# One tile for all of PSUM and a new order of work in a fused attention and MLP-mixer kernel

## The chip, the cores and the metric

The kernel runs on one core of a Trainium2 chip. The core has five engines that run their own instruction streams: TensorE (PE in the profile; its weight loads are listed as PEld), VectorE (DVE), ScalarE (ACT), GpSimd (POOL) and SyncE (SP). The metric is the device time of one execution in microseconds (us), lower is better. Before the change it is 283.89 us, the median of three runs (283.52, 283.89 and 284.70).

## The reference

The inputs are q, k and v with 8 batches, 8 heads, 576 positions and head size 64, and four weight matrices. A blockwise causal attention comes first: a position sees all positions of its own block of 64 and of earlier blocks. Its output, with the heads side by side (576 x 512 for each batch), goes through an MLP mixer: first over positions, then over channels.

```python
scores = scale * np.matmul(q, k.transpose(0, 1, 3, 2))
mask = block_i >= block_j                       # blocks of 64 positions
attn = np.exp(scores masked, less the row's maximum)
attn = attn / np.sum(attn, axis=-1, keepdims=True)
x = np.matmul(attn, v)                          # heads side by side: 8 x 576 x 512
h = np.maximum(x.transpose(0, 2, 1) @ w_tok1, 0.0) @ w_tok2   # 576 -> 256 -> 576
u = x + h.transpose(0, 2, 1)
out = u + np.maximum(u @ w_ch1, 0.0) @ w_ch2                  # 512 -> 1536 -> 512
```

## The kernel before, in words

Each batch goes through the same stages. The q and k of four heads (a head group) are loaded and turned by VectorE in 32x32 blocks (`STREAM_TRANSPOSE`, L440), so that the head dimension lies on the partitions. TensorE makes the scores from 32 rows at a time (`score_set`, L562). ScalarE takes the exponential: for the first batch over a pair of PSUM banks at once (`exp`, L580) or over one bank (L736), for later batches over one bank (L777). VectorE or GpSimd clear the masked corners (`clear`, L599) and copy a tail (L588). TensorE multiplies with v (`head_out`, L616, and `ends_out` for the last 64 positions, L669), and VectorE divides by the sums: a reciprocal and a multiply (L636 and L642, or L691 and L697). A column of ones beside v gives the sums.

Then comes the mixer: `token_up` (L814, L818, the ReLU after it at L800 or L802), for the first batch `first_u` (L849), an add of x (L862), a transpose by TensorE (L874) with the copy behind it (L393 on ScalarE, L395 on VectorE), `channel_up` (L1041) and the way back down. Other batches use forms with fewer multiplications whose lines play no part in the change.

The work is not written in the order in which it runs. Functions add operations to a list (class `Plan`, `P.add`), each with its engines, dependencies and the PSUM banks that it takes and gives back. A table of words, `ORDER` (L97 to L175), then says in which order they are issued, on which engine, and with which banks: `105Ts` is operation 105 on TensorE in the pair of banks called s, `106A` operation 106 on ScalarE. `placed()` goes through the table and emits. The engines run each its own part of that order, and wait for each other by semaphores. There are 1526 operations that are always emitted or may be.

Of PSUM's eight banks the kernel uses four as single tiles (`mm`, letters a to d) and four as two pairs (`sc`, letters s and t) for the first batch's scores. After the last pair's exponential, operation 166, the pairs are closed and four single tiles (`late`, letters e to h) opened in their place; operation 166 therefore depends also on all earlier pair exponentials.

A set of operations does nothing for the output: `raise_clock` multiplies zeros by zeros on TensorE. The first does it eleven times, 512 columns wide (L364). Another 37 (L372), of which every fourth is 256 columns wide and the others 512, may be put anywhere in the first 20 us or left out: the kernel before emits 25 of them.

GpSimd issues the loads of q, k, v and of the weights in its own order, between its other instructions: q and k (L435, L417), v (L469, one load per 128 positions, for the first batch in two head groups of five loads), the three token weights of which `w1o_sb` is a small remainder of the first (L480), and the channel weights (L503, L512). In this queue an issue sometimes waits until a load issued some places earlier has landed. The identity that TensorE's transposes use is made by GpSimd as well (masks.py).

## Time and profile before

| what | value |
| --- | --- |
| time, median of 3 runs | 283.89 us |
| span of the profiled execution | 282.2 us |
| TensorE busy | 275.3 us (98%), 3580 matmuls |
| VectorE busy | 238.8 us (85%) |
| ScalarE busy | 177.8 us (63%) |
| GpSimd busy | 78.8 us (28%) |
| moved by DMA | 31.75 MB |

The profile is of one execution; it gives its span, from the first to the last instruction, and no other time of that execution. The span is 1.7 us below the median of the runs, which also hold what lies around it. In timelines a row is a group of instructions: its start and length in us, engine, line, operation, and the result and the operands by their tiles' names; in brackets stands how long its engine was idle before it, and what ended that.

### The profile page before, as it was taken

How to read it: one execution, taken by the hardware profiler on the slowest of the kernel's cores; microseconds unless marked ns; L12 is line 12 of the kernel's file. 1: busy time of each engine (PE TensorE's matmuls, PEld its weight loads, DVE VectorE, ACT ScalarE, POOL GpSimd, SP SyncE). 2: the span in 40 equal slices, each digit the busy share in tenths (PEclk: the TensorE clock that was granted, in tenths of full speed). 3: DMA queues.
4: the chain of work that ended last, by engine and by line, in shares of the span. 5: the costliest groups of instructions: out<-in, count | busy, mean ns of one | idle time of the engine just before them, and what ended most of it. 6: DMA issues, size and time to landing. Idle time of an engine off the chain costs nothing.

```text
span 282.2 us, 8544 instructions
## 1 busy us (share of the span) xinstructions
PE 275.3 (98%) x3580; PEld 193.2 (68%) x3580; DVE 238.8 (85%) x523; ACT 177.8 (63%) x326; POOL 78.8 (28%) x131
## 2 busy tenths in 40 slices
PE   7899999999999999999999999999999999999994
PEld 2457665475768877888776658744589664788884
DVE  4589598889889989999988879887797898898974
ACT  4788888775899774899997990326840858530000
POOL 8876726371613422092257210000000000000000
PEclk9999999999999999999999999999999999999999
DMA  8999999959958947699399465150127200020555
GB/s 160 167 153 194 191 200 203 162 63 170 95 88 229 150 67 56 151 104 127 46 118 161 31 141 120 42 114 19 37 49 210 80 0 0 3 75 14 212 126 174
DMA packets 64918, 31.75 MB, mean 112 GB/s; under 512 B 53104, under 2 KB 56176, under 8 KB 64880
## 3 DMA queue, kind: packets, MB, share of 16 engines
q0 software_dynamic: 45040, 17.64, 54.0%
q1 hardware_dynamic: 19408, 12.91, 16.7%
q10 hardware_dynamic: 432, 0.66, 0.7%
q8 instruction: 28, 0.46, 0.7%
q14 instruction: 10, 0.08, 0.1%
HBM read 35.85 MB, written 9.44 MB: 160 GB/s over the span
## 4 chain that ended last, share of the span: by engine, by line
PE 82%; DMA 10%; DVE 3%; ACT 2%; POOL 1%; issue 1%; DVEq 0%; POOLq 0%
PE mm L1372 13%; PE late L1372 11%; DMA qk_sb<-in_q_dram 7%; PE late L1114 7%; PE late L1238 6%; PE mm L1114 6%; PE mm L1238 6%; PE mm L562 4%; PE late L616 3%; DMA wc_sb<-in_moe_w_ch_dram 3%; PE late L562 3%; PE late L913 3%; PE mm L814 2%; PE mm L616 2%; PE late L814 2%; PE mm L913 2%
## 5 line engine op out<-in xcount | busy, mean ns | idle before, releaser
L777 ACT ACTIVATE e_sb<-mm 128x512 bf16<-128x512 f32 x94 | 53.5, 612 | 9.8 <-PE mm L562 4.2
L777 ACT ACTIVATE e_sb<-late 128x512 bf16<-128x512 f32 x74 | 43.0, 613 | 5.6 <-PE late L562 2.7
L440 DVE STREAM_TRANSPOSE qk_sb<-qk_sb 128x288 int32<-128x288 int32 (+2 forms) x57 | 38.3, 695 | 6.0 <-ACT qk_sb L393 1.9
L469 POOL DMA_DIRECT2D vals<-in_v_dram x45 | 37.1, 833 | 8.5 <-PE late L616 7.5
L1372 PEld LDWEIGHTS <-sums 128*128 128x128 bf16 x288 | 27.8, 98 | 4.2 <-issue 0.4
L1372 PEld LDWEIGHTS <-gT 128*128 128x128 bf16 x288 | 27.9, 98 | 3.7
L562 PEld LDWEIGHTS <-qk_sb 32*64 32x64 bf16 (+1 forms) x1024 | 16.9, 99 | 16.5 <-issue 9.6
L562 PE MATMUL mm<-qk_sb 32*64 32x320 bf16 (+6 forms) x534 | 27.7, 273 | 0.0
L616 PEld LDWEIGHTS <-e_sb 128*128 128x128 bf16 x640 | 23.9, 97 | 5.4 <-issue 0.9
L393 ACT COPY late<-mm 128x512 f32<-128x512 f32 (+1 forms) x14 | 8.0, 571 | 27.6 <-DVE o_sb L1396 14.5
L562 PE MATMUL late<-qk_sb 32*64 32x320 bf16 (+6 forms) x382 | 25.0, 277 | 0.3 <-DVE x_sb L642 0.3
L1114 PEld LDWEIGHTS <-ws_sb 128*128 128x128 bf16 x192 | 17.9, 98 | 4.2 <-issue 0.9
L599 POOL MEMSET e_sb<- 64x512 bf16 (+1 forms) x23 | 11.4, 511 | 31.7 <-ACT e_sb L777 28.4
L800 ACT ACTIVATE gT<-late 128x512 bf16<-128x512 f32 x20 | 12.2, 611 | 7.4 <-PE late L1114 4.9
L1114 PEld LDWEIGHTS <-wc_sb 128*128 128x128 bf16 x144 | 15.5, 113 | 1.8
L1238 PEld LDWEIGHTS <-ws_sb 128*128 128x128 bf16 x96 | 9.4, 98 | 9.8
L616 PE MATMUL late<-vals,e_sb 128*128 128x65 bf16 x360 | 15.8, 193 | 0.0
L642 DVE TENSOR_TENSOR x_sb<-late,rinv 128x256 bf16<-128x256 f32 x36 | 14.8, 418 | 0.7
L580 ACT ACTIVATE e_sb<-sc 128x1024 bf16<-128x1024 f32 x11 | 10.8, 1026 | 4.5 <-PE sc L562 4.5
L1372 PE MATMUL mm<-wd_sb,sums 128*128 128x256 bf16 x108 | 13.1, 273 | 0.0
L616 PE MATMUL mm<-vals,e_sb 128*128 128x65 bf16 x280 | 12.4, 193 | 0.0
L417 POOL DMA_DIRECT2D qk_sb<-in_k_dram x12 | 6.6, 551 | 20.7 <-ACT e_sb L777 7.1
(203 smaller groups left out, 649.4 us busy)
## 6 DMA issues: line engine op xcount, KB each, us to landing
out_dram<-o_sb SPq DMA_DIRECT2D x14, 512.0 KB, 3.0
vals<-in_v_dram POOLq DMA_DIRECT2D x28, 128.0 KB, 5.9
qk_sb<-in_k_dram POOLq DMA_DIRECT2D x12, 288.0 KB, 5.6
qk_sb<-in_q_dram POOLq DMA_DIRECT2D x12, 288.0 KB, 6.1
wc_sb<-in_moe_w_ch_dram POOLq DMA_DIRECT2D x8, 192.0 KB, 7.8
wc_sb<-in_moe_w_ch_dram POOLq DMA_DIRECT2D x3, 512.0 KB, 8.0
out_dram<-o_sb SPq DMA_DIRECT2D x4, 256.0 KB, 3.2
vals<-in_v_dram POOLq DMA_DIRECT2D x15, 64.0 KB, 5.4
```

The costliest lines, as they stand in the source:

```text
L440: nc.vector.transpose(dst[:, 0:S, :] .rearrange("p s e -> p (s e)") .bitcast(I32) .rearrange("p (a k) -> p k a", k=NB)[:, k0:k1], raw2.bit ...
L469: nc.gpsimd.dma_start(out=t[128 - p : 128, J, hs, 0:64], in_=src)
L562: nc.tensor.matmul(out=home(n)[rows, c : c + w], lhsT=kT[i][r, 64 * j : 64 * j + keys, par], rhs=qT[i][r, 64 * q : 64 * q + w, par], start ...
L599: (nc.vector if o.engine == "DVE" else nc.gpsimd).memset(late_keys, 0.0)
L616: nc.tensor.matmul(out=u[:, I, 0:65], lhsT=e[:, h, c : c + 128], rhs=vt[:, J, head, 0:65], start=(J == 0), stop=(J == I),)
L642: nc.vector.tensor_tensor(out=xt[:, 0:4, 64 * head : 64 * head + 64], in0=u[:, :, 0:64], in1=ri[:, 0:4].to_broadcast([128, 4, 64]), op=MULT,)
L777: nc.scalar.activation(dst, bank_of(x), EXP, scale=scale)
L800: nc.scalar.activation(dst, src, RELU)
L913: nc.tensor.matmul(out=bank_of(bank), lhsT=w2_sb[:, t, 128 * si : 128 * si + 128], rhs=at[:, t, :], start=(t == 0), stop=(t == NDT - 1),)
L1114: nc.tensor.matmul(out=bank_of(bank)[:, 256 * o_ : 256 * o_ + 256], lhsT=x(o_, m), rhs=y[:, :, m, :], start=opens, stop=m == 1, skip_group ...
L1238: nc.tensor.matmul(out=bank_of(bank), lhsT=x(m), rhs=y[:, :, m, :], start=first and m == 0, stop=m == 1, skip_group_check=not first,)
L1372: nc.tensor.matmul(out=bank_of(bank)[:, 256 * i : 256 * i + 256], lhsT=x[:, kk, 128 * i : 128 * i + 128], rhs=y[:, kk], start=first and i ...
```

## The change

PSUM becomes a single tile of eight banks. A word names the bank by letters a to h; a first-batch pair takes any two neighbouring banks. The bookkeeping of pools goes, and so do operation 166's extra dependencies. The core of the diff:

```diff
-    mm = ring(4, [128, 512], FP32, "mm", psum)
-    held_banks = [tc.tile_pool(name="pairs", bufs=1, space=bass.MemoryType.PSUM)]
-    sc = ring(2, [128, 2, 512], FP32, "sc", held_banks[0].__enter__())
-    late = []
+    banks_sb = psum.tile([128, 8, 512], FP32, name="banks")
...
-    def bank_of(note):
-        if note["pool"] in EARLY:
-            return mm[note["slot"]]
-        if not late:
-            held_banks[0].__exit__(None, None, None)
-            held_banks[0] = tc.tile_pool(name="singles", bufs=1, space=bass.MemoryType.PSUM)
-            late.extend(ring(4, [128, 512], FP32, "late", held_banks[0].__enter__()))
-        return late[note["slot"]]
+    def bank_of(note, i=0):
+        return banks_sb[:, note["slot"] + i]
...
-            nc.scalar.activation(dst, sc[SC.index(note["pool"])][:, :, 0:n], EXP, scale=scale)
+            nc.scalar.activation(dst, banks_sb[:, note["slot"] : note["slot"] + 2, 0:n], EXP, scale=scale)
...
-                    late_banks = [{"pool": "late", "covers": True, "slot": i} for i in range(4)] if (j, n) == (3, 2) else None
-                    these = [exp(dst, 512, op, note, prio + 0.1 * n, urgent=2, give=late_banks, after=seen if late_banks else [])]
+                    these = [exp(dst, 512, op, note, prio + 0.1 * n, urgent=2)]
```

The table `ORDER` is written anew throughout; its first lines before and after:

```diff
-    13D 26D 24D 105Ts 106A 98Ttbc 61Td 57Td 49Td 99A 100D 30D 63Td 118A 122Ts 70Td 123A 78Td 62Td 54Td 102Tt 103A
+    22D 13D 26D 24D 43Ta 44Ta 45Ta 30D 67Ta 82P 47Ta 34P 35P 72Tg 76Tf 57Tf 70Th 32P 55Tf 48Tb 28D 59Tc 105Tc
```

The operations are the same apart from the warming ones, of which 30 in place of 25 are emitted behind the first eleven. Of the small operations that more than one engine can do, 38 go from VectorE to ScalarE, 34 the other way, 12 from VectorE to GpSimd and 9 the other way.

TensorE up to the first scores (L562 before, L527 after; `wd_sb` holds the zeros of the warming matmuls, L372 before, L343 after). The end of the warming before, and the first scores:

```order
L372 LDWEIGHTS wd_sb
L372 MATMUL mm<-wd_sb 128x512
L372 LDWEIGHTS wd_sb
L372 MATMUL mm<-wd_sb 128x512
L562 LDWEIGHTS qk_sb
L562 MATMUL sc<-qk_sb 128x512
```

and after:

```order
L343 LDWEIGHTS wd_sb
L343 MATMUL banks<-wd_sb 128x256
L343 LDWEIGHTS wd_sb
L343 MATMUL banks<-wd_sb 128x512
L343 LDWEIGHTS wd_sb
L343 MATMUL banks<-wd_sb 128x512
L343 LDWEIGHTS wd_sb
L343 MATMUL banks<-wd_sb 128x512
L527 LDWEIGHTS qk_sb
L527 MATMUL banks<-qk_sb 128x512
```

Four of these optional matmuls stand ahead of the first scores before, sixteen after; behind them come twenty-one before and fourteen after.

VectorE around the first adds of batch 0's mixer (L862 before, L824 after), whose results TensorE transposes. Before:

```order
L440 STREAM_TRANSPOSE qk_sb<-gT 128x9x32 x2
L636 RECIPROCAL rinv<-late 128x4
L642 TENSOR_TENSOR x_sb<-late,rinv 128x4x64
L440 STREAM_TRANSPOSE qk_sb<-gT 128x9x32
L636 RECIPROCAL rinv<-late 128x4
L642 TENSOR_TENSOR x_sb<-late,rinv 128x4x64
L862 TENSOR_TENSOR u_sb<-mm,x_sb 128x4x128
L862 TENSOR_TENSOR u_sb<-late,x_sb 128x4x128
```

and after:

```order
L607 TENSOR_TENSOR x_sb<-banks,rinv 128x4x64
L662 TENSOR_TENSOR x_sb<-banks,rinv 128x64
L411 STREAM_TRANSPOSE qk_sb<-gT 128x9x32
L656 RECIPROCAL rinv<-banks 128x1
L662 TENSOR_TENSOR x_sb<-banks,rinv 128x64
L411 STREAM_TRANSPOSE qk_sb<-gT 128x9x32
L824 TENSOR_TENSOR u_sb<-banks,x_sb 128x4x128
L411 STREAM_TRANSPOSE qk_sb<-gT 128x9x32
L824 TENSOR_TENSOR u_sb<-banks,x_sb 128x4x128 x2
```

The transposes of the second batch's q and k move from ahead of the last heads' division to behind it, two of them ahead of the first add.

GpSimd's queue with the values of batch 0 (`vals`), the token weights (`w_sb`, `w1o_sb`) and the first channel weights (`wc_sb`). Before:

```order
L469 DMA vals<-in_v_dram 64x4x64
L469 DMA vals<-in_v_dram 128x4x64 x4
L480 DMA w_sb<-in_moe_w_tok_dram 128x4x256
L480 DMA w_sb<-in_moe_w_tok_dram 64x256
L480 DMA w1o_sb<-in_moe_w_tok_dram 64x256
L599 MEMSET e_sb 64x2x2x64
L417 DMA gT<-in_q_dram 128x1152
L480 DMA w_sb<-in_moe_w_tok_dram 128x1152
L503 DMA wc_sb<-in_moe_w_ch_dram 128x768 x8
```

and after:

```order
L451 DMA w_sb<-in_moe_w_tok_dram 64x256
L440 DMA vals<-in_v_dram 128x4x64
L440 DMA vals<-in_v_dram 64x4x64
L451 DMA w_sb<-in_moe_w_tok_dram 128x4x256
L440 DMA vals<-in_v_dram 128x4x64
L564 MEMSET e_sb 64x2x2x64
L440 DMA vals<-in_v_dram 128x4x64
L388 DMA gT<-in_q_dram 128x1152
L564 MEMSET e_sb 64x2x2x64
L451 DMA w_sb<-in_moe_w_tok_dram 128x1152
L388 DMA gT<-in_k_dram 128x1152
L474 DMA wc_sb<-in_moe_w_ch_dram 128x768
```

The small weight `w1o_sb` goes to the place right behind the first loads of q and k, the other two parts of the first token weight go between the values, the last loads of values come behind a clear of `e_sb` and the identity, and clears stand ahead of the channel weights. Between the last two loads of values stand also the identity's three instructions, which are left out here.

More of the change, by code (lines that the diff above doesn't have):

```diff
@@ L81, in placed @@
             assert all(d.n in done for d in o.deps)
-            for letter, (pools, note) in zip(letters[1:], o.take):
-                note["pool"], note["slot"], note["home"] = pool_of[letter], self.SLOTS[letter][1], letter
-                assert letter not in held and note["pool"] in pools
-                held.add(letter)
+            for letter, (size, note) in zip(letters[1:], o.take):
+                note["slot"] = "abcdefgh".index(letter)
+                banks = range(note["slot"], note["slot"] + size)
+                assert banks.stop <= 8 and not held.intersection(banks)
+                note["whole"] = self.covered.issuperset(banks)
+                held.update(banks)
```

224 lines of the change are left out of this document (99 added, 125 removed).

## The prediction

> **What bounds the kernel now.** I read the page first (engines, clock, chain of waits), then the windows of the first 40 us, then the waits, and last each engine's timeline at the front. The page's line of engines, its clock slices and its chain:
>
> ```profile
> PE 275.3 (98%) x3580; PEld 193.2 (68%) x3580; DVE 238.8 (85%) x523; ACT 177.8 (63%) x326; POOL 78.8 (28%) x131
> PEclk9999999999999999999999999999999999999999
> PE 82%; DMA 10%; DVE 3%; ACT 2%; POOL 1%; issue 1%; DVEq 0%; POOLq 0%
> ```
>
> TensorE is busy 98% of the span and carries 82% of the chain, so the time is its work plus what it waits. The windows tell where there is anything to win (columns: the engines' busy us, the granted clock, the DMA share):
>
> ```profile
> 0.00:10.00 10.00, 7.45 (x65) 2.78 (x66) 4.59 (x13) 4.30 (x6) 8.27 (x17) 1.00 0.99 158
> 10.00:20.00 10.00, 9.88 (x159) 5.48 (x159) 7.14 (x26) 9.13 (x12) 7.67 (x13) 1.00 1.51 168
> 20.00:30.00 10.00, 9.81 (x229) 7.84 (x228) 9.55 (x30) 7.93 (x16) 7.87 (x15) 1.00 1.08 185
> 170.00:180.00 10.00, 10.00 (x138) 7.99 (x137) 8.67 (x23) 1.52 (x3) 0.00 (x0) 1.00 0.43 107
> ```
>
> Only the first stretch has real holes. From 10 to 20 us ScalarE is 9.13 busy (the first batch's exponentials), from 20 to 30 VectorE is 9.55; in the late window TensorE is full. The waits of TensorE in the whole span, shown with what released them:
>
> ```profile
> PE sc L562 <- DVE qk_sb L440: 0.9, 1, 0.9
> PE late L562 <- DVE x_sb L642: 0.3, 1, 0.3
> PE late L669 <- ACT e_sb L777: 0.2, 1, 0.2
> PE mm L814 <- DVE x_sb L642: 0.2, 1, 0.2
> ```
>
> Beyond the first scores' wait of 0.9 us, 0.7 us are left to win in waits. What decides is therefore the front, to the first channel-up matmuls of batch 0 (30 us), and whether the new order behind it stays as tight. The work behind it is the same operations, so I do not cost it one by one.
>
> **The first scores start later.** TensorE's timeline (start, time, line, operation, shape):
>
> ```profile
> 1.66 4.45 PE L364 MATMUL mm<-wd_sb 128*128 128x512 bf16 x11 [1.66 <-DVE wd_sb L339]
> 5.95 1.03 PE L372 MATMUL mm<-wd_sb 128*128 128x512 bf16 x4
> 7.86 0.88 PE L562 MATMUL sc<-qk_sb 32*128 32x512 bf16 x6 [0.89 <-DVE qk_sb L440]
> 9.02 1.04 PE L372 MATMUL mm<-wd_sb 128*128 128x512 bf16 x4
> 9.99 0.63 PE L562 MATMUL sc<-qk_sb 32*128 32x448 bf16 x8
> 10.54 0.61 PE L372 MATMUL mm<-wd_sb 128*128 128x256 bf16 x4
> 30.97 1.46 PE L1041 MATMUL mm<-uT,wc_sb 128*128 128x512 bf16 x6
> ```
>
> Four warming matmuls stand between the first eleven and the first scores now, sixteen after (fifteen 512 wide, one 256). Four of 512 take 1.03 us with a tail of about 0.17 beyond the last start, so one starts every 0.216 us; those of 256 every 0.11. From 9.02 four take until 9.88, and the scores behind them start at 9.99: going from full-array matmuls to the scores' 32-row ones costs 0.11. The sixteen end at 5.95 + 15 × 0.216 + 0.11 = 9.30, the first scores start at 9.40 instead of 7.86: **1.54 us later**. The old wait of 0.89 is covered, the rest is delay. The other side of the edit: behind the first scores twenty-one warming matmuls (twelve of 512, nine of 256) become fourteen (seven and seven, thirteen of them in the front), 3.57 us become 2.25. If TensorE alone set the pace, that would give 1.3 us back.
>
> On when the full pace begins: the eleven took 4.45 us together, 0.40 each, and the four behind them already ran at 0.216. The Trainium skill, page "TensorE: Matmul & The Clock Gate", section "The HAM clock gate (the "warmup" mystery)", says that the clock opens after a free-running window of some 3.4 us of activity and so at another moment in each run, which this one trace neither shows nor excludes. By that page an opening half a window later would slow four of the sixteen to the eleven's pace, some 0.8 us that the kernel before hides in its 0.89 us wait and the changed one would pay, and the forecast would read 286.2, an estimate from that page; the sum below does without it.
>
> **It does not give it back, since ScalarE paces that stretch.** Its timeline:
>
> ```profile
> 8.53 1.94 ACT L580 ACTIVATE e_sb<-sc 128x1024 bf16<-128x1024 f32 x2 [3.67 <-PE sc L562]
> 15.10 2.92 ACT L580 ACTIVATE e_sb<-sc 128x1024 bf16<-128x1024 f32 x3
> 18.37 1.02 ACT L580 ACTIVATE e_sb<-sc 128x1024 bf16<-128x1024 f32 x1 [0.35 <-PE sc L562]
> 19.91 1.02 ACT L580 ACTIVATE e_sb<-sc 128x1024 bf16<-128x1024 f32 x1 [0.52 <-PE sc L562]
> 22.02 0.60 ACT L777 ACTIVATE e_sb<-late 128x512 bf16<-128x512 f32 x1 [1.08 <-DVE rinv L636]
> 27.16 0.60 ACT L777 ACTIVATE e_sb<-late 128x512 bf16<-128x512 f32 x1 [0.31 <-PE late L562]
> 29.82 1.08 ACT L777 ACTIVATE e_sb<-mm 128x512 bf16<-128x512 f32 x2 [0.53 <-PE mm L562]
> 31.17 0.58 ACT L393 COPY uT<-late 128x512 bf16<-128x512 bf16 x1 [0.26 <-PE late L874]
> ...
> 32.90 0.60 ACT L800 ACTIVATE gT<-late 128x512 bf16<-128x512 f32 x1 [0.15 <-PE late L1041]
> ```
>
> From 8.53 to 18.02 it never idles: eleven exponentials of a pair of banks (about 0.96 from start to start) and two of one bank run back to back, and the warming matmuls only filled what TensorE would have waited. With scores 1.54 later, the first exponential starts at 10.07 (0.67 behind the first scores, as now). Even with no idle time the thirteen end at 20.93 − 0.35 − 0.52 + 1.54 = 21.60 rather than 20.93: **+0.67**. Removed warming inside this stretch turns into waits of the score sets for a free pair of banks, about 0.1 to 0.25 each at six sets, an estimate from stepping through the new order with these durations.
>
> **The first mixer adds of batch 0 stand behind transposes.** VectorE's timeline now:
>
> ```profile
> 25.61 0.71 DVE L440 STREAM_TRANSPOSE qk_sb<-gT 128x288 int32<-128x288 int32 x1
> 26.18 0.18 DVE L636 RECIPROCAL rinv<-late 128x4 f32<-128x4 f32 x1
> 26.40 0.43 DVE L642 TENSOR_TENSOR x_sb<-late,rinv 128x256 bf16<-128x256 f32 x1
> 26.74 0.68 DVE L862 TENSOR_TENSOR u_sb<-mm,x_sb 128x512 bf16<-128x512 f32 x1
> 27.33 0.68 DVE L862 TENSOR_TENSOR u_sb<-late,x_sb 128x512 bf16<-128x512 f32 x1
> ```
>
> All transposes of that group now stand ahead of the last heads' division, so the add L862 follows the last multiply at once. In the new order two of these transposes (0.57 from start to start) stand between the last heads and the first add, and a third between first and second add. The walk through the new rows has the first add start at about 27.3, so its result is there at 28.2, while TensorE has passed its matmuls ahead of the transposes (L874) that need it at about 27.4: a wait of 0.8, against the 0.2 and 0.2 that the front shows now. Net **+0.4**; the bounds are −0.4 (no wait at all) and +1.3 (all three transposes, 1.7, less 0.4). I take the walk's value: part of the two transposes' 1.14 us is covered by TensorE's matmuls ahead of L874.
>
> **Smaller terms.** Warming behind that point: about 0.1 more after (three of 256 against two). Changes between the scores' small-row matmuls and full ones cost 0.11 each; up to the end of the front the new order has three fewer, which stands inside the stretch that ScalarE paces and buys nothing there. Front in all: 0.67 + 0.4 + 0.1 = **+1.2**.
>
> Behind the front the new order has four fewer such changes over the whole kernel (one fewer there, −0.1), one warming matmul more (+0.1 or 0.2) and a different mix of waits. The 0.3 us of wait now seen there bounds the gain; to lose there is no bound but the VectorE's 8.67 of 10 in the late window. I put +0.3 for it, an estimate by its asymmetry: −0.4 to +2.
>
> PSUM as one tile in place of four single banks and two pairs costs no instruction: reads and writes of the same banks wait on the same operations, and counted in the two programs, TensorE's waits on ScalarE go from 193 to 220, those on VectorE from 219 to 225. A wait that is already satisfied shows no idle time in this trace. The one dependency that goes is that of the last exponential of batch 0, which waited for all earlier pairs to free the second half of the banks; it started at 19.91, 0.52 after its engine was free, put down to its own scores, so its loss buys nothing.
>
> The DMA queue of GpSimd changes too. Now, with issue times and landing:
>
> ```profile
> 11.51 3.60 POOL L469 DMA_DIRECT2D vals<-in_v_dram  x5 [0.17 <-issue]
> 16.21 0.54 POOL L480 DMA_DIRECT2D w_sb<-in_moe_w_tok_dram  x1 [0.36 <-DMA gT<-in_k_dram]
> 18.24 0.53 POOL L480 DMA_DIRECT2D w1o_sb<-in_moe_w_tok_dram  x1 [1.49 <-DMA gT<-in_k_dram]
> 20.15 3.19 POOL L503 DMA_DIRECT2D wc_sb<-in_moe_w_ch_dram  x6
> vals<-in_v_dram POOLq DMA_DIRECT2D x15, 64.0 KB, 5.4
> wc_sb<-in_moe_w_ch_dram POOLq DMA_DIRECT2D x8, 192.0 KB, 7.8
> DMA to landing us min/median/max: 4.1/5.7/8.2
> ```
>
> The small token weight w1o now goes eight loads earlier and the other two first weights before the end of the values; they are needed at 22 us, and no wait of TensorE names them now, so earlier buys nothing. Those moved back are three value loads for heads 4 to 7, one behind a clear of e_sb that waits for an exponential, and behind the identity (0.5 us): the last is issued at about 16.6 instead of 14.3, lands at 22.0 by the median of 5.4, and is read at about 23: hidden, with 1.0 us to spare. The channel weights stand behind two clears that wait for exponentials, from about 21 us; with 7.8 they land at 29 to 31, and are read from 31.1 on. Both I cost at nothing; if the cover goes, that is the fourth rival.
>
> **The sum.** 1.2 + 0.3 = +1.5 on the profiled span of 282.2, which is 1.7 below the median of the runs, 283.89: 283.7 for the span, **285.4** for the time. What the front could give without any TensorE waits: 30.97 + 1.54 − 1.32 − 0.33 − 0.4 = 30.5 for the start of those channel-up matmuls, 0.5 us earlier than now.
>
> **Rivals.** (1) The rest of the order is tighter or the front's waits vanish: the sum of the extra delay is 0 ± 0.5, 283.9. For it speaks that TensorE has 98% now and can hardly lose; against it the back-to-back exponentials. (2) Faster: ScalarE, which idles 0.35 + 0.52 + 1.08 + 0.31 + 0.53 + 0.26 + 0.15 = 3.2 us after 18 us now, runs without holes in the new order. The later start costs 1.54, so the gain is 1.66 and the time 282.2. It decides by whether the first channel-up matmuls start before 29.9; 1.08 of it is one wait for the first divisions, which the new order of head work could take away. Against it: VectorE has 9.55 busy there and stands in between. (3) Later loads: the last values land with 8.2 rather than 5.4 at 24.8, 1.8 us after they are read, or the channel weights 1 to 3 us after 31: 287 to 288.5. For it: each load waits for an earlier one of its queue to land, as the 1.49 ahead of w1o shows. (4) The "holes" to be warmed aren't slow: the granted clock is 1.00 in all windows, so warming matmuls buy no speed; this is inside my forecast, and not a case with a time of its own.
>
> **How the numbers follow.** The forecast 285.4, with its own range of 284.4 to 286.8 (front −0.4 and +0.9, rest −0.6 and +0.5): 0.56. Rival 1, 283.9: 0.13. Rival 2, 282.2: 0.14. Rival 3, 287 to 288.5: 0.17. The measurement can tell about 0.5% from no change, 1.4 us: 282.5 to 285.3. The forecast lies just beyond; its share above the bound is 0.34, below it 0.22. Slower: 0.34 + 0.17 = 0.51; the same: 0.22 + 0.13 = 0.35; faster: 0.14. The range goes from 282.2 (half of rival 2 below it) to 288.5 and, for losses in the unexamined rest, 288.8.
>
> **What would show it.** First scores at 9.3 to 9.5, preceded by no wait; exponentials from about 10.1 without idle time to 21.6; a TensorE wait of about 0.8 near 27.4, ahead of the first transposes of batch 0, released by VectorE; the first channel-up matmuls at about 31.1 instead of 29.9; from there the same distance to the end within 0.5 us. I am wrong if a first score starts before 9, if TensorE waits more than 1 us for a DMA near 22 to 31, if its waits after 40 us sum to more than 1.5, or if the clock falls under 1.00 anywhere.

## The result and the profile after

The changed kernel takes 291.06 us (median of five runs, 290.56 to 293.81) against 283.72 (283.29 to 284.70) for the kernel before on the same chip: 1.0272 times, with a 95% interval of 1.0229 to 1.0314. That is 7.3 us slower, where the prediction had 1.5. The profiled execution was the longest of the five, 293.81 us with a span of 291.7; the other four have spans of 288.4 to 289.5. All times and ratios below are of executions in the chip's faster state; one execution of f4_more_traffic, 296.66 us, was in the slower one and stands outside its time.

The page of the changed kernel, its lines of engines, clock, chain and the queue that brings instructions (packets, MB, share):

```profile
PE 279.5 (96%) x3565; PEld 195.7 (67%) x3585; DVE 242.3 (83%) x524; ACT 177.1 (61%) x322; POOL 80.2 (27%) x134
PEclk9999899999999999999999999999999999999998
q8 instruction: 28, 0.46, 0.6%
PE 84%; DVE 8%; issue 3%; ACT 3%; DVEq 0%
```

TensorE is still the engine that sets the time, at 96% instead of 98%. Two things are new. In the fifth slice, which begins at 29 us, the granted clock is below full, and "issue", time in which an engine waited for nothing that the profile shows, is 3% of the chain instead of 1%. (The last slice, also below full, lies behind the last matmul.) TensorE's waits name the place:

```profile
PE banks L811 <- issue: 1.8, 1, 1.8
PE banks L335 <- DVE wd_sb L310: 1.7, 1, 1.7
PE banks L527 <- issue: 0.7, 2, 0.4
PE banks L527 <- ACT e_sb L545: 0.6, 1, 0.6
PE banks L527 <- DVE x_sb L607: 0.2, 1, 0.2
```

The longest wait after the start is one of 1.8 us ahead of L811 that no engine and no DMA released. No line names the first mixer adds (`u_sb`, L824), for which the prediction had a wait of 0.8. TensorE's timeline at the start and around the stop:

```profile
1.66 4.87 PE L335 MATMUL banks<-wd_sb 128*128 128x512 bf16 x11 [1.66 <-DVE wd_sb L310]
6.33 3.65 PE L343 MATMUL banks<-wd_sb 128*128 128x512 bf16 x16
9.92 0.62 PE L527 MATMUL banks<-qk_sb 32*128 32x512 bf16 x4
...
31.44 0.33 PE L811 MATMUL banks<-aT,w_sb 128*128 128x128 bf16 x3
33.58 0.44 PE L811 MATMUL banks<-aT,w_sb 128*128 128x128 bf16 x5 [1.81 <-issue]
33.85 1.84 PE L1003 MATMUL banks<-uT,wc_sb 128*128 128x512 bf16 x4
```

The first scores start at 9.92, without a wait ahead of them (predicted 9.3 to 9.5). Of a row of eight matmuls in `first_u` three ran, then nothing for 1.81 us, then the other five. The four channel-up matmuls behind them took 1.84 us, where the row of four on the kernel before took 1.03 for the same shape:

```profile
29.89 1.03 PE L1041 MATMUL late<-uT,wc_sb 128*128 128x512 bf16 x4
```

The windows tell why (columns as in the prediction: the engines' busy us, then the granted clock, DMA share and GB/s):

```profile
33.00:34.00 1.00, 0.42 (x6) 0.39 (x6) 0.00 (x0) 0.39 (x1) 1.00 (x2) 0.96 1.66 141
34.00:35.00 1.00, 1.00 (x4) 0.30 (x2) 0.69 (x1) 0.00 (x0) 1.00 (x3) 0.50 1.51 107
...
37.00:38.00 1.00, 1.00 (x18) 0.53 (x19) 0.96 (x2) 0.24 (x1) 0.99 (x3) 0.83 2.41 152
```

By the trace's record of the granted clock, TensorE had half its clock from 33.92 to 37.34, 3.41 us, which costs some 1.7. So this one place cost 3.5 us in the profiled execution. ScalarE's timeline, on the other hand, has the form that was predicted, half a microsecond later:

```profile
10.58 1.02 ACT L545 ACTIVATE e_sb<-banks 128x1024 bf16<-128x1024 f32 x1 [5.81 <-PE banks L527]
...
14.35 7.47 ACT L545 ACTIVATE e_sb<-banks 128x1024 bf16<-128x1024 f32 x8
```

The thirteen exponentials of the first batch run from 10.58 to 21.82 without idle time. The end is new too. These are the last output transfers, after and before (KB each, median us from issue to landing):

```profile
out_dram<-o_sb SPq DMA_DIRECT2D x2, 128.0 KB, 2.5
out_dram<-o_sb SPq DMA_DIRECT2D x1, 256.0 KB, 3.9
out_dram<-o_sb ACTq DMA_DIRECT2D x1, 128.0 KB, 3.4
```

```profile
out_dram<-o_sb SPq DMA_DIRECT2D x2, 128.0 KB, 1.7
out_dram<-o_sb ACTq DMA_DIRECT2D x1, 128.0 KB, 1.7
```

Before, the last transfer of 128 KB lands 1.7 us after its issue; after, 3.4, in company of larger ones. From the last matmul's end to the end of the span it is 3.56 us before and 5.26 after.

To add up by stages I took the distance from each matmul's start to the next, less the usual distance for that pair of shapes. On the profiled execution the span's +9.5 is about 1.6 up to 30 us (0.7 of it a second stop like the first, at 27.4 us), 3.7 from 30 to 40 us, 2.1 from 40 to 200 us, 0.4 from 200 to the last matmul, and 1.7 after it. A few matmuls are missing in the traces (20 of 3,585 here, none on the kernel before) and were filled in for this.

### The profile page after: what moved, and what is told of

Same layout as the page of the kernel before. It is cut to its first block, busy times and chain, and to the rows that moved or that the text cites. A ratio compares the mean times of both kernels' runs of the same rounds, so it can differ in the third digit from the quotient of the medians.

```text
span 291.7 us, 8529 instructions
## 1 busy us (share of the span) xinstructions
PE 279.5 (96%) x3565; PEld 195.7 (67%) x3585; DVE 242.3 (83%) x524; ACT 177.1 (61%) x322; POOL 80.2 (27%) x134
## 4 chain that ended last, share of the span: by engine, by line
PE 84%; DVE 8%; issue 3%; ACT 3%; DVEq 0%
PE banks L1334 25%; PE banks L1200 13%; PE banks L1076 11%; PE banks L527 8%; PE banks L581 5%; PE banks L776 5%; PE banks L1003 4%; PE banks L875 3%; PE banks L1425 3%; DVE qk_sb L411 2%; ACT e_sb L545 2%; DVE x_sb L607 2%; PE banks L634 2%; PE banks L335 2%; PE banks L343 1%
## 5 line engine op out<-in xcount | busy, mean ns | idle before, releaser
L739 ACT ACTIVATE e_sb<-banks 128x512 bf16<-128x512 f32 x168 | 88.1, 610 | 23.1 <-PE banks L527 22.5
L364 ACT COPY banks<-banks 128x512 f32<-128x512 f32 x46 | 26.4, 582 | 24.2 <-PE banks L1200 10.5
L527 PE MATMUL banks<-qk_sb 32*64 32x320 bf16 (+6 forms) x1024 | 35.0, 276 | 1.5 <-issue 0.7
L527 PEld LDWEIGHTS <-qk_sb 32*64 32x64 bf16 (+1 forms) x1024 | 18.2, 100 | 16.6 <-issue 11.8
L607 DVE TENSOR_TENSOR x_sb<-banks,rinv 128x256 bf16<-128x256 f32 x64 | 26.4, 422 | 1.6
L581 PE MATMUL banks<-vals,e_sb 128*128 128x65 bf16 x640 | 26.0, 193 | 0.2
L762 ACT ACTIVATE gT<-banks 128x512 bf16<-128x512 f32 x33 | 19.4, 602 | 11.0 <-PE banks L1076 6.5
L1334 PE MATMUL banks<-wd_sb,sums 128*128 128x256 bf16 x192 | 23.6, 273 | 0.0
L1200 PE MATMUL banks<-e_sb,ws_sb 128*128 128x512 bf16 x72 | 19.5, 379 | 0.1
L1334 PE MATMUL banks<-wc_sb,gT 128*128 128x256 bf16 x144 | 17.7, 273 | 0.1
L1334 PE MATMUL banks<-wd_sb,gT 128*128 128x256 bf16 x144 | 17.7, 273 | 0.0
```

The costliest lines, as they stand in the source:

```text
L364: nc.scalar.copy(dst, src)
L527: nc.tensor.matmul(out=bank_of(*homes[n])[rows, c : c + w], lhsT=kT[i][r, 64 * j : 64 * j + keys, par], rhs=qT[i][r, 64 * q : 64 * q + w, ...
L581: nc.tensor.matmul(out=u[:, I, 0:65], lhsT=e[:, h, c : c + 128], rhs=vt[:, J, head, 0:65], start=(J == 0), stop=(J == I),)
L607: nc.vector.tensor_tensor(out=xt[:, 0:4, 64 * head : 64 * head + 64], in0=u[:, :, 0:64], in1=ri[:, 0:4].to_broadcast([128, 4, 64]), op=MULT,)
L739: nc.scalar.activation(dst, bank_of(x), EXP, scale=scale)
L762: nc.scalar.activation(dst, src, RELU)
```

## The experiments

The kernels came in four groups, e and g on one chip, f and h on two others, each group with its own runs of the kernel before (medians of 283.73 to 284.11). Ratios are what can be compared; where medians of two groups are set side by side, up to 0.4 us of the difference can be the chip's. The lines of `ORDER` wrap differently from kernel to kernel: a word like `13D` that is missing from one side here stands on the line before. "One tile" below is the kernel before with PSUM as one tile and the order otherwise untouched.

| run | time, us | before there, us | ratio (95%) |
| --- | --- | --- | --- |
| e1_one_tile | 284.59 | 284.07 | 1.003 (1.0009 to 1.0052) |
| e2_four_ahead | 289.97 | 284.07 | 1.0228 (1.0167 to 1.0289) |
| e3_tail | 290.75 | 284.07 | 1.0243 (1.0214 to 1.0272) |
| e4_four_ahead_tail | 289.19 | 284.07 | 1.0179 (1.0144 to 1.0214) |
| f1_front_before | 291.77 | 283.73 | 1.0283 (1.0249 to 1.0316) |
| f2_front_changed | 289.00 | 283.73 | 1.0178 (1.0146 to 1.0211) |
| f3_late_start | 285.54 | 283.73 | 1.0066 (1.0044 to 1.0088) |
| f4_more_traffic | 290.32 | 283.73 | 1.0208 (1.0161 to 1.0255) |
| g1_end_alone | 286.38 | 284.11 | 1.0077 (1.0055 to 1.0099) |
| g2_traffic_at_18 | 289.09 | 284.11 | 1.0172 (1.0131 to 1.0213) |
| g3_less_warming | 284.68 | 284.11 | 1.0015 (0.9997 to 1.0034) |
| g4_adds_first | 290.39 | 284.11 | 1.0215 (1.0174 to 1.0255) |
| h1_middle_from_320 | 292.33 | 284.06 | 1.0294 (1.0268 to 1.0321) |
| h2_middle_from_390 | 288.85 | 284.06 | 1.0169 (1.0144 to 1.0194) |
| h3_old_end | 289.32 | 284.06 | 1.0183 (1.0166 to 1.0200) |
| h4_changed_again | 290.36 | 284.06 | 1.0225 (1.0208 to 1.0242) |

### PSUM as one tile, and the late start

**One tile alone.** The old order, with s and t as pairs of banks e, f and g, h:

```diff
-    13D 26D 24D 105Ts 106A 98Ttbc 61Td 57Td 49Td 99A 100D 30D 63Td 118A 122Ts 70Td 123A 78Td 62Td 54Td 102Tt 103A
+    26D 24D 105Te 106A 98Tgbc 61Td 57Td 49Td 99A 100D 30D 63Td 118A 122Te 70Td 123A 78Td 62Td 54Td 102Tg 103A
```

> The order of the kernel before, unchanged, on the single tile of eight banks (pair s is banks e and f, pair t is g and h), and without the extra dependencies of operation 166. Theory: the time is lost by the new order, the single tile costs nothing: 283.7, within 0.7 of the kernel before. Rival: false dependencies on one tile cost time: 285 or more, with waits of TensorE on ScalarE or VectorE that the kernel before does not have.

1.003: 0.5 us by the medians, within the 0.7 that I called no change, but 0.9 by the ratio, whose interval leaves out 1. A small cost of the single tile is likely, and its size is not settled. The profile has a wait of 1.4 us ahead of the first scores (below), but they start at 7.83, as on the kernel before.

**Sixteen warming matmuls ahead, in the old order.** Twelve more of them between the eleven and the first scores, on one tile:

```diff
-    26D 24D 105Te 106A
+    26D 24D ... 64Ta 67Tb 71Tc 72Td 73Ta 75Tb 76Tc 77Td 105Te 106A
```

> One tile and the old order, with twelve warming matmuls more ahead of the first scores (eleven of 512, one of 256: 2.48 us at full pace), nothing else. The prediction's first term: scores at 9.4 instead of 7.9, the last exponential of batch 0 0.67 later since ScalarE has 0.9 of slack there, and by the ready slack behind it between 0.7 and 1.5 at the end: 285.2 to 286. Rival, the clock opens later in a part of the runs (5.5 to 7.2 were seen): up to 0.5 more, 286.5.

1.0066 against 1.003, which is 285.54 − 284.59 = 0.95 us if the two groups are set side by side (their kernels before differ by 0.3, and the intervals of the two ratios overlap). TensorE's timeline of e1_one_tile, then of f3_late_start:

```profile
7.83 1.22 PE L523 MATMUL banks<-qk_sb 32*128 32x512 bf16 x44 [1.38 <-DVE qk_sb L407]
```

```profile
6.30 3.51 PE L339 MATMUL banks<-wd_sb 128*128 128x512 bf16 x16
9.74 1.22 PE L523 MATMUL banks<-qk_sb 32*128 32x512 bf16 x44
```

The first scores come 1.91 us later, the last of the thirteen exponentials 1.92 later (22.81 for 20.89), the first channel-up matmuls 1.12 later (31.78 for 30.66), the end 0.95. So in the old order a late start passes whole through the exponentials, and about half of it reaches the end.

**Four ahead, in the changed order.** The opposite edit on the changed kernel:

```diff
-    26D 24D 43Ta 44Ta 45Ta 30D 67Ta 82P 47Ta 34P 35P 72Tg 76Tf 57Tf 70Th 32P 55Tf 48Tb 28D 59Tc 105Tc
+    26D 24D 30D 82P 34P 35P 32P 28D 105Tc
```

> The changed kernel without the twelve added warming matmuls ahead of the first scores (four stay). Theory of the late start: the first scores start at 7.9 in place of 9.92, and the time falls by 1.5 to 2, to about 289.3. Rival, ScalarE or the loads pace the front whenever it starts: under 0.5 is won. On the stop of 1.8 us in the middle of a row of eight matmuls: if it is a late fetch of TensorE's instructions, a stop (if one is seen) stands again at about row 958 to 960 of TensorE's program, which is now twelve matmuls further into the work, in the transposes or the scores; if it is something that these eight matmuls wait for, it stays with them, at row 934 to 936.

The first scores start at 7.74, the exponentials end at 19.78, 1.15 earlier than on the kernel before, and the time is 289.97 all the same (its executions spread from 289.08 to 293.05). TensorE's timeline shows where the lead went:

```profile
27.18 0.38 PE L523 MATMUL banks<-qk_sb 32*64 32x192 bf16 x21 [1.24 <-issue]
...
33.38 0.22 PE L832 MATMUL banks<-ident,u_sb 128*128 128x128 bf16 x1 [0.64 <-issue]
```

Again two stops that no releaser explains, now ahead of other operations: the second within the transposes L832, twelve matmuls further into the work than L811's. By the distances of the starts they cost 2.3 us together.

**Fewer warming matmuls.** The kernel before, in its own PSUM form, without the last eight (`47 59 42 66 53 60 46 44`):

```diff
-    108T 116D 117D 124D 183D 119A 162Tt 182D 160D 47Td 179D 40P 126A 138Ts 59Td 37P 42Td 109D 111Td 112T 120D 121D
+    108T 116D 117D 124D 183D 119A 162Tt 182D 160D 179D 40P 126A 138Ts 37P 109D 111Td 112T 120D 121D
```

> The kernel before, in its own two pools, without the last eight of its warming matmuls (those behind 15.9 us: five of 512, three of 256, 1.4 us of TensorE). If they only fill TensorE's waits for ScalarE: 283.8 within 0.5, the clock stays open. If they stand in the way of the score sets, as ScalarE's idle 0.35 and 0.52 behind them suggest: 0.5 to 0.9 less, 283. If the clock needs them: a share of the time at half clock near 20 us, 1.7 more.

1.0015, not to be told from 1, with the clock open from 6.39 us to the last matmul. That fits warming matmuls that only filled holes, as the prediction's fourth rival had it. The profile alone wouldn't show it: it has two waits for loads, 1.0 and 0.9 us (`w_sb`, `vals`), that the profile of the kernel before doesn't have.

### The end

**Old end on the changed kernel.** First the last 125 words in the old order and on the old engines, with and without the twelve warming matmuls ahead:

```diff
-    ... 1523A 1503S 1525S 1497D 1500T 1502S 1501D 1504A
+    ... 1499D 1503S 1521T 1500T 1522D 1501D 1525S 1504A
```

> The changed kernel with its last 125 operations (the end of the last channel-down products and the output transfers) in the order and on the engines of the kernel before; all else as changed. Theory: the last transfer leaves 0.2 us after the last add and lands 1.7 us later, not 3.4, since the transfers ahead of it are spread out again: 1.7 us less, about 289.4. Rival: the end is set by TensorE alone, and the last transfers take as long wherever they stand: 291.0 within 0.5.

> Both edits of the two runs before together. Theory: they act at the two ends and add up: 287.5 to 288. What is left over the kernel before, 3.5 to 4 us, is then the middle: the stop, TensorE's clock after it, and waits. Rival: they meet in the same slack, and the sum is less than the two by over 0.7.

e4 takes 289.19 against e2's 289.97, a gain of 0.8 whose intervals overlap; e3's ratio of 1.0243 lies 0.3% under the changed kernel's 1.0272, with overlap too. The edit brought a wait of its own near 246 us, which the waits of e3_tail name:

```profile
PE banks L1196 <- ACT banks L360: 1.0, 2, 0.7
```

With only the last 90 words that wait isn't there. This kernel ran beside the changed kernel itself:

> The changed kernel with only its last 90 operations in the old order, which leaves TensorE's order at 240 to 250 us as changed, so that the 1.0 us wait for ScalarE that the longer exchange brought with it does not arise. Theory: 1.7 to 1.8 less than the changed kernel, 289.3. Rival: as in the longer exchange, 0.3 less, 290.7.

> The changed kernel, as it is, for a second profile. Theory: a stop with no wait of its own again at rows 702 to 704 or 958 to 960 of TensorE, of another size than 0.7 and 2.0 (the other profiles with this front show 0.3 to 1.5), and no half clock unless a stop is near 2 us; span about 289. Rival: the stop belongs to the first execution only; no stop over 0.2 at these rows.

289.32 against 290.36, 1.0 us faster. From the last matmul to the end it is 3.54 us for 5.32, so 1.8 was saved there; this run's stop, 1.41 us by the distances of the starts for 0.95, took some of it back.

**The changed end alone.** One tile, old order, last 125 words as in the changed kernel:

```diff
-    ... 1499D 1503S 1521T 1500T 1522D 1501D 1525S 1504A
+    ... 1523A 1503S 1525S 1497D 1500T 1502S 1501D 1504A
```

> One tile and the old order (284.59 in its own run), with the last 125 operations in the changed order and on the changed engines. Theory: the last transfer lands 3.4 us after its issue in place of 1.7, since five of its neighbours are issued within 1.7 us; 1.7 more, 286.3. Rival: the end costs nothing by itself, as the run with the old end on the changed kernel gained only 0.3 in the times: 284.6 within 0.5.

1.0077 against 1.003: 1.8 us by the two medians, 1.3 by the ratios. From the last matmul to the end it is 4.81 us for 3.55. The issues on SyncE show the difference (start, time from the first to the last, count), g1_end_alone and then e1_one_tile:

```profile
276.46 3.22 SPq L1396 DMA_DIRECT2D out_dram<-o_sb  x4
```

```profile
275.04 4.94 SPq L1396 DMA_DIRECT2D out_dram<-o_sb  x4
```

Four issues in 3.2 us instead of 4.9, beginning later: the new order finishes more output tiles at once. That the last transfer shares the way out with them is my reading; with it goes that in the changed kernel's last microseconds 350 to 460 GB/s move without a pause, while on the kernel before the rate falls to 47 between the last transfers.

### The front, the middle and the seams

To divide the rest I put the front of one order ahead of the rest of the other (always with every operation once, so an operation that the one order did early stays early).

**The old front, 360 words, with the changed rest and end.**

```diff
-    9D 8D 14S 7D 0A ... 43Ta 44Ta 45Ta ... 369A 377A 428Ta ...
+    9D 8D 14S 7D 0A ... 105Te 106A 98Tgbc ... 93P 358P 432Tc 524D | 359P 329Tb 434Ta 355P 435D ...
```

> One tile; the first 360 words of the table in the order of the kernel before (the front, to about 40 us), the rest in the changed order, with the changed end. If the front carries the loss (late start, TensorE's stops at rows 704 and 960): the stops are gone, and what is left is the end's 1.7 and the middle's waits, which sum to 2.5 in the profile of the run with the old end: 284.6 + 4.2 = 288.8. Rival, my prediction's view that the rest behind the front costs 0.3: 284.6 + 1.7 + 0.3 = 286.6.

**The changed front, 330 words, with the old rest and end.**

```diff
-    ... 306D 369A 377A 428Ta 426Te 375A 374A ...
+    ... 306D 369A 377A 428Ta | 353D 375A 354D 350D 351D ...
```

> The mirror image: the first 330 words in the changed order, the rest in the order of the kernel before, with its end. Theory: 291.06 less 4.2 for the middle and the end, 286.9, with stops at rows 702 to 704 or 958 to 960 of TensorE where a fetch is late. Rival: the front itself costs only the predicted 1.2: 285.8. If this and the run before add up to much less than the 7 us of the whole change, the two halves meet in the same slack.

Neither divides cleanly, since the seam makes waits. The waits of f1_front_before:

```profile
PE banks L871 <- DVE u_sb L886: 1.6, 2, 0.8
PE banks L523 <- DVE o_sb L1434: 0.8, 1, 0.8
```

In f1 some 4 us are lost between 50 and 70 us, so its 291.77 says nothing of the front. In f2 two waits of 1.0 and 0.8 us for exponentials stand at 50.0 and 54.1 us, and a stop without a releaser of 1.0 ahead of L807: 289.00 − 1.8 − 1.0 = 286.2, 1.6 more than one tile's 284.59 for the changed front, with an error of the seam's size.

**The changed middle between the old front and the old end**, with the seam at 320 and at 390 words:

```diff
-    ... 446Tf 356P 378Tc 379D 387Te 388D 381Th ...
+    ... 446Tf 356P 378Tc 379D | 329Tb 94D 95D 399P 525P ...
```

> One tile; front (first 320 words) and end (last 90) in the old order, only the middle in the changed one. Theory: the many small waits of the changed middle cost 2 to 2.5, so 284.6 + 2.5 = 287, plus what the seam adds, which shows as waits within 10 us of it. Rival: the middle costs nothing by itself, 284.6 within 0.7 once the waits at the seam are taken off.

> The same with the seam after 390 words. The lower of this run and the one before is an upper bound of the cost of the changed middle: 287 by the theory, 285 by the rival.

The wait at the seam, in h1 and in h2:

```profile
PE banks L772 <- DVE x_sb L603: 2.8, 2, 2.6
```

```profile
PE banks L958 <- DVE x_sb L603: 1.9, 1, 1.9
```

h2 gives a bound, if the seam's wait is taken off whole: 288.85 − 1.9 − 284.59 = 2.4 us at most for the changed middle, and 286.8 − 1.9 − 283.4 = 1.5 by the spans of the profiled executions. By the distances of the starts from 40 to 200 us, h4_changed_again loses 2.1 us more than the kernel before and 1.6 more than one tile, with no single place above 0.45: score sets and products of the token and channel stages that start about 0.2 us late, spread over the whole stretch. What each waits for stays open, as the delays are shorter than the modelled ends of the matmuls ahead of them and so don't appear among the waits (of which from 40 to 240 us a single one of 0.2 us is listed there). h1 is worth a look for another reason, below.

### The stop that nobody releases

The changed kernel on another chip, h4_changed_again, has the stop ahead of L811 again:

```profile
1.66 3.86 PE L335 MATMUL banks<-wd_sb 128*128 128x512 bf16 x11 [1.66 <-DVE wd_sb L310]
5.36 3.51 PE L343 MATMUL banks<-wd_sb 128*128 128x512 bf16 x16
8.80 0.40 PE L527 MATMUL banks<-qk_sb 32*128 32x512 bf16 x2
...
29.96 0.33 PE L811 MATMUL banks<-aT,w_sb 128*128 128x128 bf16 x3
31.16 0.44 PE L811 MATMUL banks<-aT,w_sb 128*128 128x128 bf16 x5 [0.87 <-issue]
```

I numbered TensorE's weight loads and matmuls from the program's start. The stops stand at numbers 702 to 704 and 958 to 960, 256 apart, in every run that has them, whatever operation is there: L527 and L811 on the changed kernel, and the transposes L832 in e2, which has 24 rows fewer ahead of them. The instruction queue of the page has 28 packets and 0.46 MB, 16 KB each, for TensorE's 7,170 such rows: 256 rows a packet. The DMA view of the changed kernel from 31.2 to 32.4 us (packets, MB, share) has one such packet, beside the loads:

```profile
q0 software_dynamic: 139, 0.24, 108.6%
q8 instruction: 1, 0.02, 4.9%
```

It ran from 31.31 to 32.26, and TensorE went on at 33.58, 1.32 later. The packet ahead of it ended at 25.93, and TensorE, stopped at number 704, went on at 27.38, 1.45 later; in h4 the packet ended at 29.83 and TensorE went on at 31.16, 1.33 later. My reading, from these places and moments: TensorE has run out of instructions there. Two things decide whether it does: when the packet comes, and how soon TensorE is through with the rows before. From 448 to 704 TensorE takes about as long in either order, 5.6 us on the kernel before and 5.8 in h4, and what differs is the packet: the one behind number 448 begins 0.3 us after it on the kernel before, 2.9 in h4, which has no stop at 704, and 4.1 and 4.8 on the changed kernel and in e2, which have stops of 0.7 and 1.5 us there by the distances of the starts. It is not the changed order alone that makes it late: in f3 and g3, in the old order, it begins 2.9 us after. At 960 both play a part. From 704 to 960 the kernel before takes 8.0 us (25.88 to 33.84), since sixteen channel-up matmuls, 512 wide, lie in between; the runs with the changed front take 5.1 to 6.2 us, stops included, because that order has the narrow scores of the next batch there and the channel-up behind them. The packet behind 704 begins 2.0 to 3.3 us after it in the runs with the old front and 2.7 to 3.9 after it in those with the changed one.

The stop ahead of 960 was, by the distances of the starts, 1.97 us on the changed kernel, 0.81 in e2, 0.49 in e3, 0.27 in e4, 1.12 in f2, 1.41 in h3 and about 1.0 in h4. None of the runs with the old front (e1, f1, f3, f4, g1, g2, g3, h1, h2) has one. Two tries to steer it:

**More traffic.** My first idea was that the loads of the channel weights, dense in that window, hold the packet back. Three extra loads of 384 KB, in the old order on one tile, were meant to go out at 18 us and make the packet late:

```diff
-    39P 113D 144D 38P 36P 139A 135Tc 136D
+    39P 113D 144D 38P 36P 139A 1526S 1527S 1528S 135Tc 136D
```

> One tile and the old order, with three loads of 384 KB that nothing reads added on SyncE's queue, into the output buffers, when the twelfth exponential of batch 0 has ended (about 18 us). Theory: TensorE's instructions come in pieces of 256 rows by the same DMA engines; where these are full, a piece comes late, and TensorE stops at row 704 or 960 with no wait of its own, as in the changed kernel. At least one stop of over 0.3 us stands at row 702 to 704 or 958 to 960, with the fetch ahead of it started over 2 us after row 448 or 704. Loads that compute needs get later too, 1 to 3 us in all: 285.5 to 288. Rival: fetches are not held up by data, they start within 0.5 of row 448 as now, and only the waits for loads named as DMA grow.

The experiment missed: SyncE issued them at 1.7 us, as nothing held them, so the first loads of q and k came late. Its waits:

```profile
PE banks L523 <- DVE qk_sb L407: 3.4, 1, 3.4
PE banks L577 <- DVE aT L760: 1.0, 1, 1.0
```

The second try held them by a small VectorE clear of the target:

```diff
-    161P
+    1526D 1527S 1528D 1529S 1530D 1531S 82P 161P
```

> One tile and the old order, with the three loads of 384 KB that nothing reads, this time held by a write of VectorE until about 18 us, so that they fill the DMA engines between 19 and 26 us (the lull of 70 to 130 GB/s at 19 to 21 us goes). Theory: the fetch of TensorE's instructions that starts within 0.5 us of row 448 now starts 2 to 5 us after it, and the one of row 704 too; a stop with no wait of its own at row 704 or 960 if the landing is later than 1.4 us ahead of it. Loads that compute needs get later also: in all 1 to 5 us. Rival: the fetch starts within 0.5 us of row 448 as before, and only waits for loads grow.

This time the traffic rose to 365 GB/s between 23 and 24 us and was 260 and 264 from 27 to 29 us, where e1_one_tile has 204 and 216, and the packet behind number 704 began 2.0 us after it, as in e1_one_tile. So more bytes there didn't delay the packet, and that theory isn't borne out. It isn't excluded either: the DMA engines' busy share in these windows, 1.07 to 1.15, is that of e1_one_tile (1.10 to 1.17), so the edit did not make them fuller. What it did cost is in the waits, a weight that TensorE needs:

```profile
PE banks L999 <- DMA wc_sb<-in_moe_w_ch_dram: 1.7, 1, 1.7
PE banks L832 <- POOL ident masks.py:199: 0.7, 1, 0.7
```

**The adds first.** The changed kernel with the three transposes of the next batch moved behind the second mixer add:

```diff
-    212A 173D 174D 177D 268A 189D 89P 156D 157D 58Tb 195Tcbdh 199A 271Tg 272A 185D
-    274D 277Ta 186D 207P 275Tf 269Te 196A 197A 278D 270A 276A 285Tc 286D
+    212A 173D 174D 177D 268A 89P 156D 157D 58Tb 195Tcbdh 199A 271Tg 272A
+    274D 277Ta 207P 275Tf 269Te 196A 197A 278D 189D 185D 186D 270A 276A 285Tc 286D
```

> The changed kernel with the three transposes of the second batch moved from around the first adds of the mixer to behind the second add. My prediction's second term (TensorE waits 0.8 for the first add): 0.4 to 0.8 less, 290.4. What the trace of the changed kernel shows (the transposes that need the add start without idle time): no difference within 0.5, 291, or some more, since the scores that need these transposes come later.

1.0215, the same as h4's 1.0225. The stop at 960 is gone, since another wait takes its place, 1.1 us long and ahead of it, for those transposes:

```profile
PE banks L523 <- DVE qk_sb L407: 1.1, 1, 1.1
```

So moving the adds ahead won nothing: the changed order has at most 0.2 us of wait for them, and the edit brings a wait of its own. And a stretch that was held up by a microsecond before number 960 has no stop there. What sets the moment at which a packet's transfer begins stays open; it was not moved by intent in any run.

### The parts together

On h4, whose clock stayed open to the last matmul, the span is 5.6 longer than the kernel before's 282.2: 0.76 in the front without the stop, 0.95 for the stop, 2.1 in the middle and 1.8 after the last matmul. The two profiles of the changed kernel differ by how long the stops are and whether the clock closes behind them. No kernel of this study was faster than the kernel before.

## Why the prediction was wrong

- **First scores 1.54 later: right in mechanism, the size varies.** Predicted 9.40; measured 9.92 on the changed kernel, 8.80 in h4, with the same sixteen warming matmuls ahead. The moment at which the clock opens sets it, by the trace's record of it: 6.62 us in the one, 4.35 in the other. A warming matmul takes 0.40 us before that moment and 0.216 after it, so 2.27 us of later opening should cost about half of that, and 1.12 was measured; g4 lies between (5.20 and 9.22). This is what the Trainium skill, page "TensorE: Matmul & The Clock Gate", section "The HAM clock gate (the "warmup" mystery)", says of the opening, which the sum left out; the trace agrees, with a wider spread than the half microsecond given there.
- **+0.67 at the last exponential: right on the changed kernel's first profile, not on its second.** There is no idle time in either, as predicted. The first ends at 21.82 where 21.60 was predicted, 0.89 later than before. In h4 the eight last of the thirteen end at 20.70, 0.23 earlier than before, since the clock opened early:

```profile
13.23 7.47 ACT L545 ACTIVATE e_sb<-banks 128x1024 bf16<-128x1024 f32 x8
```

  So this term is not what makes h4 slow. (The prediction's "eleven exponentials of a pair" up to 18.02 are nine; with the two behind them they are eleven.) Alone, in the old order, a start 1.91 us later cost 0.95 at the end (f3 against e1).
- **+0.4 for the wait for the first mixer add: absent.** TensorE's matmuls ahead of its transposes lasted long enough; at most 0.2 us of wait for the adds shows in any run of the changed order, and moving the adds ahead gave nothing.
- **The front in all, +1.2: measured 0.76 in h4 and 1.1 on the changed kernel, without the stops.** The size was about right by luck: the second term was absent, and the first had the other sign in h4.
- **First channel-up at 31.1: it was 33.85, in h4 31.44.** What stood between is the stops, 2.7 us on the changed kernel and about 1.0 in h4. The prediction had no term for them. The walk through the new order had priced every wait that one instruction has for another, and none for the arrival of the instructions themselves, as the trace of before has no such stop.
- **+0.3 for the rest (−0.4 to +2): this is the term of the sum that failed.** The middle cost 1.5 to 2.4 and the end 1.0 to 1.8 (in h4 by its span, 2.1 + 1.8 = 3.9, beyond the bound of 2). For the end the cause is shown by exchanging it both ways; what delays the middle stays open. "The work behind it is the same operations, so I do not cost it one by one" was the choice behind it. The end could have been read from the order: its output issues stand closer together, and the last transfer is on the path with nothing behind it to hide it.
- **One tile at nothing:** 0.5 us by the medians, 0.3 to 1.5 by the interval of the ratio.
- **Rivals.** (2), ScalarE without holes in the first batch's exponentials, happened on the changed kernel itself, and in e2 with exponentials ending 1.15 us earlier than before, and gained nothing: TensorE's stops took the lead. (3), late loads (which the paragraph on the loads calls the fourth rival), didn't happen; on the changed kernel no wait for a DMA stands among TensorE's. (4), no gain from warming, is borne out by g3 for the last eight. Its reason does not hold: a clock of 1.00 in the window from 0 to 10 us counts only from the opening, at 5.55 us, and the eleven ran at 0.40 us each before.
- **What I said would make me wrong:** a first score did start before 9 (8.80 in h4), the clock under 1.00 did occur, and the losses after 40 us exceeded 1.5, though as delays too short for the list of waits, and behind the last matmul, where that list has nothing.

The single experiments do not add up to a sum: f3's 0.95 belongs to a start 1.91 us later, while h4's is 0.94 later, and h2's 2.4 for the middle is a bound. The division that closes is that of h4's span, 5.6 us as given above; by the medians on that chip it is 6.3. Of the first comparison's 7.3, a difference of medians, the low clock explains nothing: only the profiled execution can have had it. A low stretch of 3.41 us takes 0.006 off an execution's mean clock, and the other four have means of 0.996 and 0.997. What makes their median 0.7 longer than h4's was not traced.

## What to carry to other kernels

When an order written for tightness is replaced as a whole, price its end and its even middle as well as the place where the change is visible: the end here cost more than the late start, and it is read from how many output transfers are issued in the last microseconds. A stretch of many very short matmuls can be too fast for its own instructions; where the profile shows a wait with "issue" in a constant distance of instructions, look at the instruction queue's packets. Spreading long matmuls among short ones should help by the times above; no run here tried it. Warming work put ahead of the first useful work delays what follows: in f3, 1.91 us at the first scores were 1.92 at the last exponential and about half of that at the end.

## What the runs showed of the hardware

- **TensorE's instructions come in packets of 256.** TensorE stopped at numbers 704 and 960 for 0.3 to 2.0 us, and went on 1.3 to 1.6 us after a packet's end. The runs with the old front, which take 7.6 us or more from 704 to 960, have no stop at 960.
- **The clock fell to half around a stop of under 2 us, and it changes on a grid of 3.41 us.** On the changed kernel it fell to 0.50 for 3.41 us, 0.34 us after the end of the stop of 1.81. In h1 it fell at 49.47, 1.1 us into the wait of 2.6 us, and stayed low for 6.8 us, to 56.30; its windows around the fall:

```profile
48.00:50.00 2.00, 0.37 (x10) 0.28 (x10) 1.97 (x5) 0.00 (x0) 0.00 (x0) 0.87 1.16 210
50.00:52.00 2.00, 0.79 (x2) 0.40 (x3) 0.87 (x4) 0.00 (x0) 0.00 (x0) 0.50 1.09 208
```

  In f4 TensorE was idle for 3.38 us, from 6.9 to 10.3 us, and the clock stayed open:

```profile
8.00:9.00 1.00, 0.00 (x0) 0.00 (x0) 0.72 (x1) 0.00 (x0) 0.47 (x1) 1.00 1.24 308
```

  The same section of the page "TensorE: Matmul & The Clock Gate" of the Trainium skill has the clock throttled after at least one idle window of about 3.4 us. The length of the low clock here, 3.41 us, agrees with such a window. The record shows more: in all 18 profiles the clock changes a whole number of 3.413 us after the opening (8 of them on the changed kernel, 13 in h1, 81 to 83 where it closed only at the end). Counted in such stretches, f4's idle time lay in two, 1.94 us in the first and 1.44 in the second, and the changed kernel's stop lay whole in the one from 30.51 to 33.92, which has 1.84 us of idle time in all. That 1.84 closed the clock and 1.94 did not doesn't follow from idle time alone, and a wholly idle stretch was not needed; the measurement decides. What else counts stays open. The stretch that closed held mostly scores on 32 of the 128 rows, f4's first one six matmuls of 128 rows, 512 wide.
- **The clock opens at very different moments.** Over the 18 profiles of this study it opened between 4.35 and 7.69 us, with matmuls running from 1.66 us in all of them, so 2.7 to 6.0 us after their start.
